# Attention output: all state products ahead of the chunk products, one open group per column group of a bank

## The chip, the cores and the metric

The kernel runs on one core of one Trainium2 chip. The metric is device time in microseconds of that core. Before the change the median of 13 runs is 155.75 us (154.82 to 157.44). A profile is one execution recorded by the hardware profiler; its span is the time from the first to the last instruction.

## The reference

Two parts follow each other. The first is a gated linear recurrence for 4 batches of 8 heads, 768 tokens and head size 48; its output, laid out as 3072 tokens of 384 features, goes into a feed-forward layer with the maximum of three products:

```python
state = zeros(B, H, 48, 48)
for t in range(768):
    state = alpha[:, :, t, :, None] * state + k[:, :, t, :, None] * v[:, :, t, None, :]
    y[:, :, t] = einsum('bhd,bhde->bhe', q[:, :, t], state)
x = y as (3072, 384)
h = maximum(maximum(x @ w1, x @ w2), x @ w3)      # 768 wide
out = h @ w_out                                   # 384 wide
```

## The kernel before

The tokens are cut into 12 steps of 256: step s is chunk s // 4 of batch s % 4. A step has two row blocks of 128 tokens (x = 0 and 1), and within them tokens go in pairs. For one row block the attention output is a sum of two kinds of products: the scaled queries with the state that stands before the block (its state products), and the masked scores within the block with the values (its chunk products). The first row block of chunk 0 has no state yet, so it has chunk products alone.

The work on a step is cut into pieces, each a small function with a letter: sums of logarithms of the gates (`c`), their exponentials, scaled queries and keys (`k`, `q`), their transposes, on TensorE for the first steps (`T`) and by DMA on the SP queue from step 5 on (`D`), scores (`A`), the mask (`a`, VectorE), the attention output (`Y`, the function `attend`), its copy to SBUF (`x`, `keep_x`), the new state (`S` on TensorE, `s` on VectorE, `z` mostly on GpSimd), and the feed-forward part: gate products (`G`), maxima (`h`), the last product (`O`) and the store (`o`). Three strings, PROLOGUE, STEADY and LAST, give the order in which the pieces are written out by hand; each engine runs its own instructions in that order, and waits only for data and for buffers. STEADY is written out once per stage and interleaves the feed-forward part of one step with the attention of the next and the preparation of the ones after it.

PSUM has eight banks, given out under three tags: `w` (2), `s` (2) and `g` (4). `attend` takes two banks of one tag, one for each row block, `yps[x]`. A bank holds the output turned round, as 128 partitions by three groups of 128 tokens. The 128 partitions are four column groups of 32 (m), and each of the three groups f of a column group is one block of 32 output features. A block of 32 features lies in the 48 of one head or reaches into the next one: `part` 0, 1 or 2 within a pair of heads. `turns[m]` is the order in which the column group m takes its three f; the block that reaches over two heads comes second.

A state product (line 311) multiplies 128 rows by 32 columns of the state with 128 tokens of queries. A chunk product (line 330) multiplies 64 rows by 32 columns of the values with 128 columns of the masked scores; x chooses the upper or lower 64 rows. A late attend (chunk 1 and 2, eight of them) has 24 state products and 64 chunk products; an early one (chunk 0, four) has 12 and 64. The function writes them in this order: state products of the first group of each column group, then the chunk products that close the first group and open the second, then the state products that close the second group and those that open the third, and then the chunk products that close the third. In each column group of a bank one accumulation group is open at a time: the first product onto a group has `start`, the last has `stop`.

Of the kernel before, what the change touches and what calls it, by code (L numbers as in the profile page):

```python
# [23 lines left out]
def kernel(  # L24
# [12 lines left out]
    nc = tc.nc  # L37

    B, H, S, D = q.shape
    NT, DM = out.shape  # L40
    DF = moe_w_out.shape[0]
    P = 128
    C = 32
    NF = DM // P
    NJ = DF // P
    U = 2
    R = 2
    J = P // R
# [3 lines left out]
    HP = H // 2  # L52
# [120 lines left out]
    def bank(shape, name, tag, dtype=FP32):  # L173
        return ps.tile(shape, dtype, name=name, tag=tag, bufs=banks[tag])
# [116 lines left out]
    def attend(s, _, tag):  # L291
        c, b = divmod(s, B)
        vt, qkT = vts[s % NQ], qkT_of.pop(s)
        lats = [lat_of.pop((s, u)) for u in range(U)]
        yps = [bank([P, NF, P], "yps", tag or "s") for _ in range(U)]
        for x in range(U):
            y_of[s, x] = yps[x]
        blocks = [divmod(n, 3) for n in range(NF * P // C)]
        old = [U * c + x > 0 for x in range(U)]

        turns = []
        for m in range(P // C):
            fs = sorted(range(NF), key=lambda f: blocks[P // C * f + m][1] == 1)
            turns.append([fs[0], fs[2], fs[1]])

        def from_state(g, first):
            for x in range(U):
                for m in range(P // C) if old[x] else ():
                    f = turns[m][g]
                    p, part = blocks[P // C * f + m]  # L310
                    nc.tensor.matmul(yps[x][C * m:C * (m + 1), f, :],  # L311
                                     sts[b][x][:, p, C * part:C * (part + 1)],
                                     qkT[:, :, 0, p, x * J:(x + 1) * J], start=first, stop=not first)

        def from_chunk(*groups):
            jobs = []
            for m in range(P // C):
                todo = []
                for g, first in groups:
                    f = turns[m][g]  # L320
                    p, part = blocks[P // C * f + m]
                    cols = [(0, C * part)] * (part < 2) + [(1, D + C * (part - 1))] * (part > 0)
                    todo += [(f, first, n == 0, n == R * len(cols) - 1, i, p, n % R, at)
                             for n, (i, at) in enumerate(j for j in cols for _ in range(R))]
                jobs.append(todo)
            for n in range(max(len(j) for j in jobs)):
                for m, job in enumerate(jobs):
                    for x in range(U) if n < len(job) else ():
                        (f, first, begin, end, i, p, r, at), rows = job[n], slice(x * J, (x + 1) * J)
                        nc.tensor.matmul(  # L330
                            yps[x][C * m:C * (m + 1), f, :],
                            vt[rows, r * HP + p].rearrange("p a b -> p (a b)")[:, at:at + C],
                            lats[p // (HP // R)][rows, i, p % (HP // R) * R + r, :],
                            start=begin and (first or not old[x]),
                            stop=end and (not first or not old[x]))

        from_state(0, True)
        from_chunk((0, False), (1, True))
        from_state(1, False)
        from_state(2, True)  # L340
        from_chunk((2, False),)

    def keep_x(s, x, eng):
        if s not in xT_of:
# [92 lines left out]
    def warm(_, n, *x):  # L437
# [9 lines left out]
        "k": scale_k, "q": scale_q, "V": values,  # L447
        "T": turn, "t": keep_turned, "D": turn_by_dma, "A": scores, "a": masked,
        "Y": attend, "x": keep_x, "M": gates, "S": update, "s": add_state, "z": decay_state,
        "G": gate, "h": maxed, "O": project, "o": store,  # L450
    }
# [95 lines left out]
```

## Time and profile before

| What | Value |
|---|---|
| median of 13 runs | 155.75 us |
| profiled execution, its own time | 155.98 us |
| its span | 154.2 us |
| TensorE busy | 144.8 us (94%) |
| VectorE busy | 120.7 us (78%) |
| GpSimd busy | 84.8 us (55%) |
| ScalarE busy | 77.7 us (50%) |
| chunk products of attend, L330 | 768, busy 11.0 us |
| state products of attend, L311 | 240, busy 7.8 us |
| gate products, L396 | 648, busy 78.0 us |
| granted TensorE clock | 1.00 throughout |

In lines of the profile PE is the matmul side of TensorE, PEld its weight loads, DVE is VectorE, ACT ScalarE, POOL GpSimd, SP SyncE, which here only issues DMAs (SPq). L330 is line 330 of the kernel. A line of a timeline gives a start, a length, the operation, output<-inputs and a count, and in brackets the idle time before it and what ended it. Matmuls overlap, and each one's end is modelled, so a sum of busy times by line can be more than what the line adds to the time; the chain of work that ended last counts each moment once.

### The profile page before, as it was taken

To read this page: it belongs to the slowest core of one execution; us is meant where nothing else is said; L and a number is where in the kernel's file an instruction comes from. 1 tells how busy PE (TensorE), PEld (TensorE's weight loads), DVE (VectorE), ACT (ScalarE), POOL (GpSimd) and SP (SyncE) were. 2 spreads that over 40 slices of the span, in tenths; PEclk is the share of its full clock that TensorE was granted. 3 is DMA by queue.
4 is the path that set the end of the run, shared out by engine and by line. 5 is a ranking of instruction groups with operands and counts; after the bars stand their busy time and mean duration, and the time that the engine had idled before them with its cause. 6 is when DMAs were issued, how large, how long until landed. Compare 5 with 4: busy or idle time off the path is not lost.

```text
span 154.2 us, 6225 instructions
## 1 busy us (share of the span) xinstructions
PE 144.8 (94%) x2691; PEld 108.1 (70%) x2691; DVE 120.7 (78%) x212; ACT 77.7 (50%) x156; POOL 84.8 (55%) x123
## 2 busy tenths in 40 slices
PE   6989883999999999999999999999999999999990
PEld 2446452788877698687787786886877878868850
DVE  2256985699989799989799799797896995885560
ACT  3578927645774386383582483553835614132221
POOL 5418798466919307928848659379288573010000
PEclk9999999999999999999999999999999999999999
DMA  5999998799999999799999999999908609411023
GB/s 138 322 325 325 277 330 253 229 351 285 361 284 249 234 320 296 208 123 284 261 237 283 167 218 334 141 261 294 234 5 82 160 4 106 137 55 51 6 100 104
DMA packets 73035, 32.52 MB, mean 211 GB/s; under 512 B 65456, under 2 KB 73008, under 8 KB 73008
## 3 DMA queue, kind: packets, MB, share of 16 engines
q1 hardware_dynamic: 72576, 31.89, 83.2%
q8 instruction: 21, 0.34, 1.0%
q10 hardware_dynamic: 432, 0.23, 0.6%
q14 instruction: 6, 0.05, 0.1%
HBM read 23.73 MB, written 4.72 MB: 184 GB/s over the span
## 4 chain that ended last, share of the span: by engine, by line
PE 84%; DVE 4%; DMA 3%; issue 2%; SPq 2%; POOL 1%; ACT 1%; ACTq 0%; POOLq 0%
PE gps L396 48%; PE ops L420 15%; PE yps L330 6%; PE yps L311 4%; PE aps L280 4%; PE sps L369 3%; DMA ra<-in_alpha_dram 3%; PE tps L259 2%; SPq L95 2%; DVE lat L287 2%; POOL qk L235 1%; PE wps L440 1%; PE lps L209 1%; DVE pa L184 1%; ACT ob L156 1%
## 5 line engine op out<-in xcount | busy, mean ns | idle before, releaser
L396 PE MATMUL gps<-xT,wcat 128*128 128x256 f16 x648 | 78.0, 273 | 0.2 <-DVE lat L287 0.2
L396 PEld LDWEIGHTS <-wcat 128*128 128x128 f16 x648 | 60.8, 98 | 10.5 <-ACT wcat L150 0.7
L411 DVE TENSOR_TENSOR hT<-gps,h 128x512 f16<-128x512 f32 x36 | 24.4, 687 | 11.3 <-PE gps L396 11.1
L287 DVE TENSOR_TENSOR lat<-aps,cp 128x512 f16<-128x512 f32 x48 | 30.6, 682 | 1.7 <-PE aps L280 1.7
L156 ACT ACTIVATE ob<-ops,c 128x384 f32<-128x384 f32 (+1 forms) x21 | 12.1, 574 | 38.0 <-PE ops L420 37.2
L411 DVE TENSOR_TENSOR h<-gps,h 128x512 f16<-128x512 f32 x36 | 24.1, 688 | 3.4 <-PE gps L396 1.2
L420 PE MATMUL ops<-wo,hT 128*128 128x384 f16 x144 | 26.5, 326 | 0.0
L383 POOL TENSOR_TENSOR st<-full,gm 128x384 f16<-128x384 f32 x20 | 16.9, 846 | 15.7 <-DVE full L379 10.0
L420 PEld LDWEIGHTS <-hT 128*128 128x128 f16 x144 | 14.1, 98 | 7.3 <-DVE hT L411 0.2
L353 POOL TENSOR_TENSOR gt<-ge 128x4 f32<-128x4 f32 x17 | 4.2, 248 | 21.3 <-ACT ge L229 21.3
L150 ACT CAST xT<-yps 128x384 f16<-128x384 f32 x21 | 9.2, 481 | 11.9 <-PE yps L330 11.7
L152 DVE CAST h<-gps 128x512 f16<-128x512 f32 x20 | 13.7, 687 | 1.2 <-PE gps L396 1.1
L150 ACT CAST h<-gps 128x512 f16<-128x512 f32 x16 | 9.3, 586 | 10.4 <-PE gps L396 7.2
L440 PE MATMUL wps<-blank 128*128 128x512 f16 x47 | 13.1, 426 | 1.2 <-DVE blank L512 1.2
L330 PE MATMUL yps<-lat,vt 64*32 64x128 f16 x768 | 11.0, 220 | 2.2 <-issue 2.2
L235 POOL TENSOR_TENSOR qk<-ka,ic 128x384 f16<-128x384 f32 x11 | 11.4, 1035 | 0.3 <-ACT ic L217 0.2
L235 POOL TENSOR_TENSOR qk<-qa,ac 128x384 f16<-128x384 f32 x11 | 11.0, 998 | 0.2
L156 ACT ACTIVATE vt<-rv,c 128x768 f16<-128x768 f32 x11 | 10.3, 938 | 1.3 <-DMA rv<-in_v_dram 1.3
L184 POOL TENSOR_TENSOR pa<-ra 128x384 f32<-128x384 f32 x9 | 9.0, 1001 | 3.5 <-DVE ka L199 3.5
L330 PEld LDWEIGHTS <-vt 64*32 64x32 f16 x768 | 7.2, 90 | 4.7 <-issue 2.4
L235 POOL TENSOR_TENSOR qk<-rq,ac 128x384 f16<-128x384 f32 x10 | 10.0, 999 | 0.0
L440 PEld LDWEIGHTS <-blank 128*128 128x128 f16 x47 | 4.6, 107 | 6.6 <-issue 2.4
(52 smaller groups left out, 166.5 us busy)
## 6 DMA issues: line engine op xcount, KB each, us to landing
ra<-in_alpha_dram SPq DMA_DIRECT2D x12, 384.0 KB, 5.6
rk<-in_k_dram SPq DMA_DIRECT2D x12, 384.0 KB, 5.1
rq<-in_q_dram SPq DMA_DIRECT2D x12, 384.0 KB, 5.4
rv<-in_v_dram SPq DMA_DIRECT2D x12, 384.0 KB, 5.4
out_dram<-ob SPq DMA_DIRECT2D x23, 192.0 KB, 3.9
ws<-in_moe_w_dram SPq DMA_DIRECT2D x9, 384.0 KB, 6.4
ws<-in_moe_w_out_dram SPq DMA_DIRECT2D x3, 384.0 KB, 4.9
qkT<-qk SPq DMA_TRANSPOSE x14, 4.6
```

The costliest lines, as they stand in the source:

```text
L150: nc.scalar.copy(out=dst, in_=src)
L152: engines[eng].tensor_copy(out=dst, in_=src)
L156: nc.scalar.mul(dst, src, col)
L184: engines[eng or "p"].tensor_mul(pair_of[s], raw("a", s, 0), raw("a", s, 1))
L235: engines[eng or "p"].tensor_mul(dst.rearrange("p a b c -> p (a b) c")[:, :, :D], near_of.pop((s, n)) if r == 0 else raw(n, s, 1), dec_of[ ...
L287: nc.vector.tensor_mul(lat_of[s, u][:, i].rearrange("p (a r) t -> p a r t", r=R), aps_of[s, u][i].rearrange("p (a r) t -> p a r t", r=R), ...
L330: nc.tensor.matmul(yps[x][C * m:C * (m + 1), f, :], vt[rows, r * HP + p].rearrange("p a b -> p (a b)")[:, at:at + C], lats[p // (HP // R)] ...
L383: engines[eng or "p"].tensor_mul(sts[s % B][1 - x].rearrange("p a (b d) -> p a b d", d=D), full_of.pop((s, x)), gm_of.pop((s, x)).unsqueez ...
L396: nc.tensor.matmul(gps[:, j, :], wcat[:, f, g, jj * P:(jj + 1) * P], xT[:, f].rearrange("p u t -> p (u t)"), start=(f == 0), stop=(f == NF ...
L411: nc.vector.tensor_max(h, gps, h_of[s, i - 1])
L420: nc.tensor.matmul(ops, hT_of[s][:, jj, u * P:(u + 1) * P], wo16[:, jj, :], start=(jj == 0), stop=(jj == NJ - 1))
L440: nc.tensor.matmul(wps, blank[:, :P], blank, start=True, stop=True)
```

## The change

The state products of all three groups are written first, for row block 0 and then 1, and then all chunk products in one run. Within a column group of a bank only the very first product has `start` (the state product of the first group, or the first chunk product where there is no state), and only the very last has `stop`: all three groups f of a column group are open together. The argument `skip_group_check` changes no instruction. The order of chunk products is the same as before within the run, and so is their number.

```diff
-        def from_state(g, first):
-            for x in range(U):
-                for m in range(P // C) if old[x] else ():
+        for x in range(U):
+            for g in range(NF) if old[x] else ():
+                for m in range(P // C):
                     f = turns[m][g]
                     p, part = blocks[P // C * f + m]
                     nc.tensor.matmul(yps[x][C * m:C * (m + 1), f, :],
                                      sts[b][x][:, p, C * part:C * (part + 1)],
-                                     qkT[:, :, 0, p, x * J:(x + 1) * J], start=first, stop=not first)
-
-        def from_chunk(*groups):
-            jobs = []
-            for m in range(P // C):
-                todo = []
-                for g, first in groups:
-                    f = turns[m][g]
...
-                        nc.tensor.matmul(
-                            yps[x][C * m:C * (m + 1), f, :],
-                            vt[rows, r * HP + p].rearrange("p a b -> p (a b)")[:, at:at + C],
-                            lats[p // (HP // R)][rows, i, p % (HP // R) * R + r, :],
-                            start=begin and (first or not old[x]),
-                            stop=end and (not first or not old[x]))
-
-        from_state(0, True)
-        from_chunk((0, False), (1, True))
-        from_state(1, False)
-        from_state(2, True)
-        from_chunk((2, False),)
+                                     qkT[:, :, 0, p, x * J:(x + 1) * J], start=(g == 0), stop=False, skip_group_check=True)
+
+        jobs = []
+        for m in range(P // C):
+            todo = []
+            for f in turns[m]:
...
+        for n in range(max(len(j) for j in jobs)):
+            for m, job in enumerate(jobs):
+                for x in range(U) if n < len(job) else ():
+                    (f, i, p, r, at), rows = job[n], slice(x * J, (x + 1) * J)
+                    nc.tensor.matmul(
+                        yps[x][C * m:C * (m + 1), f, :],
+                        vt[rows, r * HP + p].rearrange("p a b -> p (a b)")[:, at:at + C],
+                        lats[p // (HP // R)][rows, i, p % (HP // R) * R + r, :],
+                        start=(n == 0 and not old[x]), stop=(n == len(job) - 1),
+                        skip_group_check=True)
```

## The prediction

> **What bounds the kernel now.** I read the page's busy shares first, then the chain of work that ended last, then the stages one by one. Before has a median of 155.75 us; its profiled execution took 155.98 us and its span is 154.2 us, so 1.8 us lie around the span. All sums below are made in the span.
>
> ```profile
> span 154.2 us, 6225 instructions
> PE 144.8 (94%) x2691; PEld 108.1 (70%) x2691; DVE 120.7 (78%) x212; ACT 77.7 (50%) x156; POOL 84.8 (55%) x123
> PE 84%; DVE 4%; DMA 3%; issue 2%; SPq 2%; POOL 1%; ACT 1%; ACTq 0%; POOLq 0%
> ```
>
> TensorE carries the end: it is busy for 94% of the span and holds 84% of the chain. Attend runs twelve times, once per step. In the chain its state products (L311) and chunk products (L330) are separate pieces. This is the chain (start us, length us, what) in a late attend with both row blocks old:
>
> ```profile
> 84.22 0.97 PE ops L420 x6
> 85.19 0.23 PE yps L311 x8
> 85.42 0.53 PE yps L330 x48
> 85.95 0.34 PE yps L311 x16
> 86.29 0.23 PE yps L330 x16
> 86.52 2.07 PE gps L396 x18
> ```
>
> The attend costs 1.33 us in four blocks with no gap before or after. The same chain in the third attend, where only x=1 has a state:
>
> ```profile
> 38.97 0.17 PE yps L311 x4
> 39.14 0.53 PE yps L330 x48
> 39.67 0.23 PE yps L311 x8
> 39.89 0.24 PE yps L330 x16
> ```
>
> From these lengths a block's cost splits in two. State blocks of 4, 8 and 16 take 0.17, 0.23 and 0.34 us: 14 to 15 ns per product, and 0.11 to 0.12 us whatever the count. Chunk blocks of 16 and 48 take 0.235 and 0.53 us: 9.2 ns per product, and 0.09 us whatever the count. The trace's single starts say the same: within a block, rounds of four (state) or eight (chunk) products start 56 to 75 ns apart, and from the last start of one kind to the first weight load of the other pass about 0.15 us (85.726 to 85.878, 86.067 to 86.214).
>
> Then the stretches between attends, for slack (us, then busy us of each engine):
>
> ```profile
> core 0: us, PE busy (x) PEld busy (x) DVE busy (x) ACT busy (x) POOL busy (x), PEclk, DMA share, GB/s
> 85.19:95.75 10.56, 10.56 (x228) 8.25 (x231) 9.41 (x17) 5.60 (x12) 7.24 (x12) 1.00 1.09 230
> ```
>
> TensorE is busy for the whole of each stage from 39 us on, and the stages from 64 to 127 us are all 10.56 to 10.58 us long. VectorE is next with 9.41 us. The waits of the stage before this one show that it stands still for TensorE once, for 1.0 us:
>
> ```profile
> DVE hT L411 <- PE gps L396: 1.0, 1, 1.0
> ```
>
> Three places of the first third differ. TensorE's timeline after the first attend (it ends at 20.0) and inside the second, and VectorE's after the third:
>
> ```profile
> 21.91 0.40 PE L259 MATMUL tps<-cp,qk 128*128 128x128 f16 x4 [0.56 <-POOL qk L235]
> 24.32 0.41 PE L330 MATMUL yps<-lat,vt 64*32 64x128 f16 x29
> 26.91 0.34 PE L330 MATMUL yps<-lat,vt 64*32 64x128 f16 x19 [2.18 <-issue]
> 42.29 0.68 DVE L411 TENSOR_TENSOR hT<-gps,h 128x512 f16<-128x512 f32 x1
> 43.13 0.69 DVE L411 TENSOR_TENSOR h<-gps,h 128x512 f16<-128x512 f32 x1 [0.17 <-PE gps L396]
> ```
>
> After the first attend TensorE waits for GpSimd. The second is cut by 2.18 us in which TensorE waits for nothing the profile shows. After the third, VectorE works without a pause from 34.0 to 43.0 us, and TensorE's gate product at 43.1 follows hT closely.
>
> **What the Trainium skill says.** TensorEngine Tiling (Array Packing), Tiling Modes, Key Properties: changing the tiling mode, not merely the tile, drains the TensorE. State products are 128 rows by 32 columns, chunk products 64 by 32, so each border between blocks is such a change; the trace agrees, with 0.15 us at the border against 0.056 us between rounds. PSUM — Partial Sum Buffer, The four PSUM rules: the start flag clears the written-bits of the whole bank in the quadrants written, and later products without it overwrite where the bit is clear and add where it is set; so one start per column group and bank suffices, and the flags themselves carry no work. No run here shows that rule by itself. The Performance Considerations of the first page give a fixed overhead of about 60 cycles per matmul; the trace's spacing is used instead.
>
> **The change part by part.** No instruction is added or removed: the order has the same 2691 matmuls and as many weight loads, and the other engines' and SP's orders are the same but for line numbers. Waits sit on the corresponding instructions.
>
> State groups 1 and 2 move ahead of all chunk products: 16 in the eight late attends, 8 in the four early ones. Four blocks become two. Late attend: 24 state products, 0.34 + 8 x 0.0145 = 0.45 us; 64 chunk products, 0.53 + 16 x 0.0092 = 0.68 us; together 1.13 against 1.33, a gain of 0.20 us, which is one state block's and one chunk block's fixed part (0.115 + 0.09). Early attend: 12 state, 0.23 + 4 x 0.0145 = 0.29, and 64 chunk, 0.68: 0.97 against 1.17, again 0.20 us.
>
> One uncertainty is the slope in a run of 64. In the 48-block the first four rounds start 56 to 66 ns apart, the later ones about 67 to 75 with the instructions evenly 4.2 ns apart, as if supply ran out. Two more rounds at 56 give 0.64, at 75 give 0.68. I take 0.68, the dearer; the other end adds 0.04 us per attend. A second is x: before, the 16-block alternates banks; after, x=0 writes three rounds into its own bank before x=1 starts. The third attend's 8-block (x=1 alone, one bank) and the late 8-block (x=0, then x=1) both take 0.23 us, so I price this at nothing, and it can hardly be below.
>
> Waits: the moved state products read the state and qkT that group 0 has waited for already. x=1's first state product now stands 8 products later, the first chunk product 16 later, so their waits for st, the yps bank and lat are looser. What waits for an attend is keep_x (ScalarE, then gate), and both yps banks still end with the last chunk products: it moves as a whole. No DMA is issued by attend; the transposes and loads on SP follow GpSimd and other consumers, which follow TensorE.
>
> Does the gain last to the end? I compared, for each TensorE wait, the producer's end with the waiter's start; a truly blocked one starts 0.05 us after. In a late stage the nearest is the project bank freed by add_state (0.29 us), which follows TensorE's own update, begun 1.5 us earlier, so it moves along; VectorE regains step at its 1.0 us wait. The transposes (landing 0.18 us before their reader in the stage at 102 us, 0.6 to 1.9 in the others) lose 0.2 us of their room: perhaps 0.1 us once. Early: first attend, gain 0 (GpSimd's 0.56 us wait takes it). Second: 0.20, since the two borders that go lie after the stall. Third: hT ends 0.115 us before its reader, so 0.06. Fourth: 0.20. Sum: 0 + 0.20 + 0.06 + 0.20 + 8 x 0.20 = 2.06. The transpose may take 0.1 from it and the cheaper end of the chunk slope add up to 0.4 (ten attends by 0.04); I leave both out and take 2.05. Span 152.15; the profiled execution's 155.98 becomes 153.9, and the median of the runs 155.75 becomes **153.7 us**.
>
> **The rivals.** (1) DMA or VectorE takes most of it. DMA share reads 0.98 to 1.12 in the four stages from 64 to 106 us, and VectorE is at 89%. If each of those four stages keeps its 10.56 us, 0.8 us are lost, and with the second attend's gain lost too, 1.0: about 154.7. Against it: SP's queue stands idle for 1.0 to 1.5 us ahead of each later pair of transposes, because it waits for GpSimd and not for room.
> (2) The change doesn't do what it says: the border costs are moved into the longer blocks (64 chunk products starve for instructions, all rounds at about 90 ns instead of 67, 8 x 23 ns = 0.18 us). Then 155.6, the same. The measured 67 to 75 in rounds five and six speaks against more.
> (3) Slower: three rounds running into one bank serialize. A late attend has 4 such neighbours among its six rounds. At 50 ns each the 0.20 us is gone; at 75 ns (so 131 in place of 56) a late attend loses 0.10 us and eight lose 0.8; an early one, with 2 neighbours, still gains 0.05, so about 156.4. The 0.23 us of both 8-blocks speaks against it.
>
> **How the numbers follow.** Forecast 0.72, rival 1 0.15, rival 2 0.07, rival 3 0.06. A measurement here can tell about 0.5% (0.8 us) from no change: below 154.97 is faster. Of the forecast nearly all and of rival 1 about two thirds are faster: 0.81. Same 0.12, slower 0.07. The forecast's own range is 153.0 (chunk slope at the cheap end, and run to run 0.3) to 154.4; taking in rival 1, 80% lie between 152.9 and 155.0.
>
> **What would show it.** In the chain, each late attend as two pieces, x24 of 0.45 and x64 of 0.64 to 0.68 us, and the stages from 74 us at 10.36 us with TensorE still fully busy. After the first attend a longer wait for GpSimd, and near 43 us a wait of about 0.15 us for hT. Wrong if state pieces of 24 last over 0.6 us, if TensorE shows waits in the late stages, or if the stall in the second attend changes its length: nothing in the waits says what sets it, it lies ahead of both borders that go, and at over 4.2 us it would use up the whole gain.

## The result, and the profile after

The changed kernel took 154.0 us (median of 11 runs, 153.14 to 156.47) against 155.94 us (48 runs) of the kernel before. Medians take in all executions; ratios leave out those, of any kernel, that took over 1.5% more than its fastest. The ratio is 0.9901, with a 95% interval of 0.9873 to 0.993. That is 1.5 us faster (1.1 to 2.0). The forecast was 153.7 us and a gain of 2.05 us: the direction and the place are right, and the size is a little high. Two later sets of runs of the same kernel gave 0.9872 (0.9802 to 0.9943) and 0.9855 (0.9796 to 0.9913).

The profiled execution of the changed kernel took 154.98 us, 1.0 us more than its median, so its span (153.2 us) shows more losses than a usual run. The lines of the page that answer to those of before:

```profile
span 153.2 us, 6225 instructions
PE 143.2 (93%) x2691; PEld 108.3 (71%) x2691; DVE 121.9 (80%) x212; ACT 77.6 (51%) x156; POOL 84.5 (55%) x123
PE 65%; DVE 12%; DMA 7%; POOL 5%; issue 4%; SPq 2%; ACT 2%; ACTq 0%; DVEq 0%; POOLq 0%
```

TensorE still bounds the kernel, but its share of the chain fell from 84% to 65%: the chain now runs for longer through VectorE (12%), DMAs (7%) and GpSimd (5%). The same chain in a late attend (L311 state products, L328 chunk products, L388 gate products):

```profile
82.73 0.98 PE ops L412 x6
83.70 0.45 PE yps L311 x24
84.15 0.66 PE yps L328 x64
84.82 2.08 PE gps L388 x18
```

Two pieces instead of four, and 1.11 us instead of 1.33. The weight loads of TensorE in the same place show the two blocks as the engine sees them:

```profile
83.63 0.34 PEld L311 LDWEIGHTS <-st 128*32 128x32 f16 x24 [0.32 <-issue]
84.08 0.60 PEld L328 LDWEIGHTS <-vt 64*32 64x32 f16 x64
84.74 0.33 PEld L388 LDWEIGHTS <-wcat 128*128 128x128 f16 x4
```

A stage between two attends (columns as before):

```profile
73.29:83.63 10.34, 10.34 (x224) 8.26 (x223) 9.41 (x17) 5.60 (x12) 7.22 (x12) 1.00 1.07 239
```

It is 10.34 us long instead of 10.56, TensorE is busy for all of it, and VectorE and GpSimd do the same work as before in the shorter time.

Not all stages are so. TensorE's timeline has these stops after the start of the second attend (in brackets the idle time and what ended it):

```profile
25.85 0.56 PE L328 MATMUL yps<-lat,vt 64*32 64x128 f16 x43 [1.00 <-issue]
41.97 1.47 PE L388 MATMUL gps<-xT,wcat 128*128 128x256 f16 x12 [0.24 <-DVE hT L403]
95.43 0.36 PE L328 MATMUL yps<-lat,vt 64*32 64x128 f16 x22 [0.45 <-issue]
102.20 0.64 PE L280 MATMUL aps<-qkT 48*64 48x128 f16 x32 [1.00 <-DMA qkT<-qk]
```

The first stop is the one that before has in its second attend, shorter this time. The second was forecast (0.15 us for hT). The third and the fourth are new: in the eighth attend TensorE stands still after 42 chunk products, and seven microseconds later the scores wait 1.0 us for a transpose by DMA. The two take 1.45 us, more than twice the 0.66 us that the three stages from 63 to 94 us gained: the changed kernel starts its eighth attend 1.7 us ahead of before (93.98 against 95.68 us) and its ninth only 0.1 us ahead (106.14 against 106.26).

### The profile page after: what moved, and what is told of

The parts are those of the page before. It is cut to its first block, busy times and chain, and to the rows that moved or that the text cites. A ratio compares the mean times of both kernels' runs of the same rounds, so it can differ in the third digit from the quotient of the medians.

```text
span 153.2 us, 6225 instructions
## 1 busy us (share of the span) xinstructions
PE 143.2 (93%) x2691; PEld 108.3 (71%) x2691; DVE 121.9 (80%) x212; ACT 77.6 (51%) x156; POOL 84.5 (55%) x123
## 4 chain that ended last, share of the span: by engine, by line
PE 65%; DVE 12%; DMA 7%; POOL 5%; issue 4%; SPq 2%; ACT 2%; ACTq 0%; DVEq 0%; POOLq 0%
PE gps L388 35%; PE ops L412 13%; PE yps L328 4%; DMA qkT<-qk 4%; PE aps L280 3%; POOL qk L235 3%; DMA ra<-in_alpha_dram 3%; DVE hT L403 3%; PE yps L311 2%; SPq L95 2%; PE sps L361 2%; DVE lat L287 2%; DVE h L403 2%; PE tps L259 2%; PE wps L432 2%
## 5 line engine op out<-in xcount | busy, mean ns | idle before, releaser
L388 PE MATMUL gps<-xT,wcat 128*128 128x256 f16 x648 | 78.0, 273 | 0.2 <-DVE hT L403 0.2
L388 PEld LDWEIGHTS <-wcat 128*128 128x128 f16 x648 | 60.9, 98 | 10.0 <-PE gps L388 0.5
L432 PE MATMUL wps<-blank 128*128 128x512 f16 x47 | 13.6, 439 | 1.2 <-DVE blank L504 1.2
L328 PE MATMUL yps<-lat,vt 64*32 64x128 f16 x768 | 9.2, 221 | 1.5 <-issue 1.5
L280 PE MATMUL aps<-qkT 48*64 48x128 f16 x384 | 8.6, 218 | 1.4 <-DMA qkT<-qk 1.0
```

Source lines behind the costliest of these rows:

```text
L280: nc.tensor.matmul(aps[i][cols, a * R + r, :], qkT[rows, r, 1, p, cols], qkT[rows, :, 0, p, cols], start=True, stop=True)
L328: nc.tensor.matmul(yps[x][C * m:C * (m + 1), f, :], vt[rows, r * HP + p].rearrange("p a b -> p (a b)")[:, at:at + C], lats[p // (HP // R)] ...
L388: nc.tensor.matmul(gps[:, j, :], wcat[:, f, g, jj * P:(jj + 1) * P], xT[:, f].rearrange("p u t -> p (u t)"), start=(f == 0), stop=(f == NF ...
L432: nc.tensor.matmul(wps, blank[:, :P], blank, start=True, stop=True)
```

## The experiments

Two theories and their rivals were put to test. The **border theory**: what costs is each passage from state to chunk products and back, whatever the number of products and whatever groups are open. The **transfer theory**: the part of the gain that was missing went to the transposes by DMA, which no longer land ahead of their readers. A third, on TensorE's own instructions, came out of the traces.

| Run | What it is | Median us | Ratio to before (95%) |
|---|---|---|---|
| changed kernel | two blocks | 154.0 | 0.9901 (0.9873 to 0.993) |
| e1_after_again | the same | 154.06 | 0.9872 (0.9802 to 0.9943) |
| e2_six_blocks | six blocks | 157.49 | 1.0132 (1.005 to 1.0215) |
| e3_four_blocks_two_open | four blocks, two open groups | 155.96 | 0.9975 (0.9944 to 1.0006) |
| e4_one_in_middle | two blocks and one product between | 155.64 | 0.9983 (0.9954 to 1.0012) |
| e5_warm_halves | changed, 47 more matmuls ahead | 156.05 | 1.0007 (0.9966 to 1.0048) |
| e6_q0_early | changed, earlier transposes | 153.32 | 0.9819 (0.979 to 0.9848) |
| e7_banks_alternate | changed, banks alternate | 154.02 | 0.9836 (0.9794 to 0.9879) |
| e8_before_q0_early | before, earlier transposes | 155.8 | 0.9999 (0.9963 to 1.0035) |
| e9_q0_early_again | e6 again | 153.98 | 0.9883 (0.9835 to 0.9931) |
| e10_after_third | changed kernel again | 153.65 | 0.9855 (0.9796 to 0.9913) |

e1 to e4 shared runs of before (median 156.15), e5 to e7 (156.0), and e8 to e10 (156.69).

**Borders: two more.** Before, with the middle chunk block parted:

```diff
         from_state(0, True)
-        from_chunk((0, False), (1, True))
-        from_state(1, False)
+        from_chunk((0, False),)
+        from_state(1, True)
+        from_chunk((1, False),)
         from_state(2, True)
         from_chunk((2, False),)
```

> Before with the chunk products of the first and second group parted by the second group's state products: six blocks per attend instead of four, one group open at a time. Border theory: 0.20 us more per attend where TensorE sets the time (9 to 11 of 12): plus 1.8 to 2.2 us, ratio 1.012 to 1.014, late attends of 1.53 us. Rival (what is saved by the change comes with the open groups or the start flags): as before, ratio 1.000.

It became 1.3% slower (2.1 us; 0.8 to 3.4), as the border theory has it. The chain of a late attend:

```profile
117.39 0.23 PE yps L311 x8
117.61 0.24 PE yps L330 x16
117.85 0.22 PE yps L311 x8
118.07 0.35 PE yps L330 x32
118.42 0.23 PE yps L311 x8
118.64 0.24 PE yps L330 x16
```

The same products take 1.51 us in six blocks, 1.33 in four and 1.11 in two: 0.18 and 0.22 us for each pair of borders. Open groups and flags can't have cost this: the kernel has one open group per column group at a time, like before. Whether they save anything is the question of the next run.

**Open groups without fewer borders.** The same four blocks, but the first two groups open together:

```diff
         from_state(0, True)
-        from_chunk((0, False), (1, True))
         from_state(1, False)
+        from_chunk((0, False), (1, False))
         from_state(2, True)
         from_chunk((2, False),)
```

(with `stop` and the group argument as in the changed kernel)

> State products of the first and second group ahead, then their chunk products, then the third group's state and chunk products: two groups open together, still four blocks. Border theory: ratio 1.000 (0.997 to 1.003), late attends of 1.33 us as x16, x48, x8, x16. Rival (open groups, start flags): a good part of the gain, 0.993 to 0.995.

The ratio is 0.9975, and its interval reaches into what the rival expected; the chain decides:

```profile
104.79 0.34 PE yps L311 x16
105.12 0.53 PE yps L331 x48
105.66 0.23 PE yps L311 x8
105.88 0.24 PE yps L331 x16
```

It is 1.33 us, as before, with the sizes of the two state blocks exchanged. Two groups open in a bank save nothing by themselves.

**One product in the middle.** The changed kernel, with the last state product of row block 1 left out of the first block and written after half of the chunk products:

```diff
+        places = [(x, g, m) for x in range(U) for g in range(NF) for m in range(P // C)]
+        from_state([i for i in places if i != last])
...
         for n in range(max(len(j) for j in jobs)):
+            if n == 4:
+                from_state([last])
```

> The changed kernel with one of its 24 (or 12) state products per attend, the last, moved into the middle of the chunk products: the order is as in the changed kernel but for this one, and two borders are back. Border theory with a cost that does not depend on the count: 0.20 us more per attend than the changed kernel, ratio to before 0.998 to 1.002. Rival (the cost goes with the number of moved products or with the groups): nearly the whole gain stays, 0.988 to 0.993.

```profile
105.80 0.44 PE yps L313 x23
106.25 0.35 PE yps L334 x32
106.59 0.16 PE yps L313
106.75 0.35 PE yps L334 x32
```

One product out of 24 gives back nearly all that the change saves: 1.30 us, and a ratio of 0.9983. The lone product holds TensorE for 0.16 us in the chain, and parting the chunk block costs 0.04 on top (two of 0.35 against one of 0.66). Here the cost does not go with the count.

Is it the change of tile shape that costs, or any change from one kind of product to another? The trace of before has both. Gate products (L396) and last products (L420) are both 128*128 tiles, score products (L280) are 48*64:

```profile
81.38 0.45 PE aps L280 x32
81.83 0.76 PE gps L396 x6
82.59 0.98 PE ops L420 x6
83.56 0.66 PE gps L396 x6
```

Six gate products take 0.66 us after last products and 0.76 us after score products. Between single starts it is the same: from a gate product to a last product pass 0.109 us, which is the spacing of gate products themselves, but from a last product to the first state product (128*32) pass 0.256 us, where last products are 0.162 us apart. Score products follow products of the new state (64*64, L369) after 0.033 us, so 48 rows in place of 64 cost nothing either. In this trace, then, passages that keep the 128*128 or the 64*64 tile are free, and those to another tile cost about 0.1 us or more. This fits what the Trainium skill states (TensorEngine Tiling (Array Packing), Key Properties, cited in the prediction): a change of the tiling mode drains TensorE. The drain itself no trace shows.

**Banks.** The changed kernel with the loops over groups and row blocks exchanged:

```diff
-        for x in range(U):
-            for g in range(NF) if old[x] else ():
-                for m in range(P // C):
+        for g in range(NF):
+            for x in range(U):
+                for m in range(P // C) if old[x] else ():
```

> The changed kernel with the loops over groups and row blocks exchanged in the state products: neighbouring rounds of four write banks 0, 1, 0, 1 instead of 0, 0, 0, 1, 1, 1. Border theory: nothing changes, x24 in 0.45 us and the ratio of the changed kernel (0.985 to 0.993). Rival (rounds into one bank hinder each other): x24 shorter by 0.05 us or more in late attends, 0.4 us in all.

```profile
105.70 0.45 PE yps L311 x24
106.15 0.67 PE yps L328 x64
```

The 24 state products take 0.45 us in either order, so rounds into one bank do not hinder each other (rival 3 of the prediction). Its ratio overlaps with those of the changed kernel.

**The missing part: transposes.** The changed kernel once more, unedited:

> The changed kernel once more, for a second profile. Border theory (each pair of borders between state and chunk products costs 0.20 us): late attends again as x24 of 0.45 and x64 of 0.66 us, stages of 10.35 us, ratio 0.985 to 0.993. Transfer theory for the part of the gain that the first profile lost (1.0 us at 102 us, waiting for a transpose by DMA): TensorE waits again for a transpose by 0.3 us or more in some stage from 70 to 134 us. Its rival, chance: no such wait over 0.3 us, and that profile's 1.0 us was one run's.

The attends are again x24 of 0.45 and x64 of 0.67. In this profile the scores at 82.3 us start 0.29 us late and 0.13 us after a transpose landed, as in the first profile (102.07 to 102.20 us); the timeline names VectorE there, but its result was there earlier. So it just missed the 0.3 us that the transfer theory asked for. Then GpSimd's order was changed, so that the first transpose of a stage can be issued earlier:

```diff
-        h1@0 h5@0 V0@2 k0p@2 S0@1 s0@1 z0p@1 A0g@1 a0@1 A1@1 k1p@2 G7@0
-        O1@-1 a3@1 G6@0 q0p@2 s1@1 q1p@2 a1@1 a2@1 D0@2 D1@2 l3@5 l1@5
+        h1@0 h5@0 V0@2 k0p@2 S0@1 s0@1 z0p@1 A0g@1 a0@1 A1@1 q0p@2 G7@0
+        O1@-1 a3@1 G6@0 k1p@2 s1@1 q1p@2 a1@1 a2@1 D0@2 D1@2 l3@5 l1@5
```

> The changed kernel with two of GpSimd's pieces in the steady stages exchanged: the scaled queries of the first token come before the scaled keys of the second, so the first of the two transposes by DMA can be issued some 0.95 us earlier in a stage and the second some 0.6 us. Transfer theory (the transposes set part of the time since the change): they land 0.6 us or more earlier ahead of their readers, no wait of TensorE for them is left, ratio 0.001 to 0.004 better than the changed kernel. Rival (the DMA engines' queue and not the issue decides when they land, or the wait was chance): room and time as in the changed kernel.

No wait for a transpose was left. Of the seven pairs, the second transpose landed 1.0 to 2.3 us ahead of its reader. The ratio was 0.9819, better than any of the changed kernel. To see what belongs to the exchange, it was then run on before, and again beside the changed kernel:

> Before with GpSimd's exchange alone (scaled queries of the first token ahead of the scaled keys of the second). Transfer theory: in before the transposes land ahead of their readers already (0.18 to 1.9 us), so they get room that nobody needs: ratio 0.997 to 1.002; the exchange is worth something only after the borders are gone. Rival (the exchange helps by itself, through GpSimd or VectorE): as much as it gave the changed kernel, 0.990 to 0.995.

> The changed kernel with the exchange, once more beside the changed kernel itself, for the size: transfer theory 0.3 to 1.0 us faster than the changed kernel, ratio to before 0.980 to 0.986, and no wait of TensorE for a transpose. Rival (the first reading was chance): the ratio of the changed kernel, 0.987 to 0.990.

> The changed kernel beside the two above. Border and transfer theory: ratio 0.985 to 0.990; a wait of TensorE for a transpose in one of the stages from 70 to 134 us in about half of the profiles (two of the four so far of kernels with two borders fewer and without the exchange). If instead the time is that of the exchange's kernel, the transposes cost nothing.

On before it is worth nothing (0.9999), as expected. The second set of runs of the exchange gave 0.9883, no better than the changed kernel beside it (0.9855), and the medians were 153.98 and 153.65 us. So the first reading was in part chance, and whether the exchange makes the changed kernel faster stays open. The waits say a little more. The changed kernel's third profile had its stop again, in another stage:

```profile
80.08 0.64 PE L280 MATMUL aps<-qkT 48*64 48x128 f16 x32 [0.47 <-DMA qkT<-qk]
```

Over all profiles: of the five with two blocks and GpSimd's old order (the changed kernel three times, e5, e7) four have one wait for a transpose, of 1.00, 0.29, 0.64 and 0.47 us; I had counted only two of the first four when I wrote the last expectation. Of the two with the exchange none has one, and none of the five with four or six blocks has. So the wait came with the shorter stages; it is 0.5 us on average over the five, and none has it twice. That the exchange takes it away rests on two profiles, and in the second of these the closest transpose landed 0.4 us ahead of its reader.

**TensorE's own instructions.** The stops that wait for nothing shown stand at fixed places of the instruction stream. In the changed kernel's first two profiles they follow the 350th and the 1756th matmul, 1406 apart. TensorE has 5382 matmuls and weight loads. The page lists an instruction queue with 21 packets (q8), which I take for TensorE's, as it has by far the most instructions. A packet then stands for about 256 instructions or 128 matmuls, and 1406 is 11 of these within two; the packets ahead of the two stops are 11 apart as well. In all twelve profiles the stop at the 350th matmul ends 2.3 to 2.6 us after one of these packets begins (23.42 to 25.85 us in the changed kernel, 24.36 to 26.91 in before), and the one at the 1756th likewise (93.06 to 95.43). To tell the place in the stream from the place in the attend, each warm-up matmul was written as two halves:

```diff
-        for _ in range(n):
-            nc.tensor.matmul(wps, blank[:, :P], blank, start=True, stop=True)
+        for _ in range(2 * n):
+            nc.tensor.matmul(wps[:, :256], blank[:, :P], blank[:, :256], start=True, stop=True)
```

> The changed kernel with each of the 47 warm-up matmuls of 512 columns written as two of 256, so that every later instruction of TensorE stands 47 matmuls (94 instructions) further on in its stream, at the same work. In both profiles of the changed kernel TensorE stood still, waiting for nothing shown, after its 350th matmul (in the second attend) and after its 1756th (in the eighth, after 42 chunk products, 0.4 us in the matmul row), 1406 matmuls or 11 times 256 instructions apart. Supply theory (TensorE's own instructions come late, in portions of 256): the standstills stay at counts near 350 and 1756, so they leave the places they had, the second attend and the 42nd chunk product of the eighth; 0.3 to 1.5 us faster than the changed kernel if the new places are less dense. Rival (a run of 64 chunk products itself stalls): the eighth attend still stalls after some 42 chunk products, time unchanged.

The timeline ahead of the second attend, and the eighth attend:

```profile
23.02 0.36 PE L280 MATMUL aps<-qkT 48*64 48x128 f16 x12
27.38 0.32 PE L280 MATMUL aps<-qkT 48*64 48x128 f16 x4 [4.00 <-issue]
...
99.04 0.52 PE L311 MATMUL yps<-qkT,st 128*32 128x128 f16 x24
99.49 0.74 PE L328 MATMUL yps<-lat,vt 64*32 64x128 f16 x64
100.16 1.05 PE L388 MATMUL gps<-xT,wcat 128*128 128x256 f16 x8
```

The first stop stayed at the 350th matmul, which is now a score product ahead of the second attend. So its place belongs to the stream and not to the work. The eighth attend runs through, and so does the 1756th matmul; but e7 and e10, with the changed kernel's count of instructions, show no such stop there either (e7 a delay of 0.2 us), so on the second stop e5 decides nothing. That a run of 64 chunk products does not stall by itself is seen in every profile, in all the attends that run through.

The hoped-for gain did not come: the whole gain of the change was gone (1.0007). Two things came together. In the profiled execution, at 158.24 us the longest of the 14, the stop lasted 4.0 us, because its packet began 1.4 us after TensorE had stopped (24.81 us). And 2.1 us into the stop, at 25.48 us, the granted clock fell to half, until 32.31 us; the page shows it in slices of 3.9 us:

```profile
PEclk9999997589999999999999999999999999999998
28.46 1.49 PE L388 MATMUL gps<-xT,wcat 128*128 128x256 f16 x6
```

Six gate products take 1.49 us there, against 0.66 at full clock. TensorE worked for 4.9 us at half the clock, which costs up to 2.5 us by my estimate (half of 4.9). This is not that one execution alone: in 12 of the 14 the mean granted clock was 0.972 to 0.989, against 0.994 or more in all but one of the changed kernel's executions; and the two at 0.997 and 0.999 took 154.98 and 154.39 us, less than the other twelve. So part of the loss goes with the lower clock, and how much the place of the stop costs without it stays open. So does what decides when a packet begins.

## Why the prediction came out as it did

**The attend: right.** Forecast 1.13 us for a late attend, measured 1.11 to 1.12, and 0.95 against 0.97 for an early one; the slope for 64 chunk products lay at 0.66 to 0.67, between the ends of 0.64 and 0.68. The fixed parts of the blocks, read from the chain of before, are the cause: e2, e3 and e4 show them each in its own way.

**The stages: right.** From the start of the fourth attend to the end of the span, before takes 102.15 us, and e3 and e8 102.3 and 102.1; the three two-block profiles without a wait for a transpose (e5, e6, e9) take 100.2 to 100.4. That is 1.8 to 1.95 us for nine attends, against 9 x 0.20 in the sum. The prediction named waits of TensorE in the late stages and another length of the stall as signs of being wrong. Both came (1.0 us at 102 us; 1.0 us in place of 2.18), but they are what follows below, and not a fault in what a border costs.

**The transposes: the term that was mis-sized.** The sum left them out ("perhaps 0.1 us once"), on one profile's smallest room of 0.18 us. Four of five profiles have a wait of 0.29 to 1.00 us, 0.5 us on average over the five. The reasoning that the room shrinks by 0.2 us was sound. But the 0.18 us were no room: in all four stops TensorE's wait instruction for the transpose passes 0.03 us after the landing and the matmul follows 0.13 us after it, and in before, at 102 us, the wait passes 0.03 us after the landing too. And the room itself varies by about a microsecond from run to run: in this stage of the first two profiles the second transpose landed at 102.10 us (before) and at 102.07 us (after), though it was issued 0.8 us earlier in the latter (97.14 and 96.37). Rival 1 came near this: it had DMAs take back up to 1.0 us, but through four stages that keep their whole length. Those stages did get shorter; a single late transpose was what cost, and VectorE had no part in it in the late stages.

**The early part: right in three of four attends.** The first gained nothing. The second gained 0.2 us: from its start to the third, less the stop, 12.35 us in before and 12.16 in e6, e7, e9 and e10. The first profile of the changed kernel has 12.31 there, and e1 12.76, with a wait of 0.37 us for VectorE in it. The third was put at 0.06, and its wait for hT, forecast as about 0.15 us, is there in all seven two-block profiles, at 0.22 to 0.26 us. From the third to the fourth, before takes 13.15 us; e5, e7 and e9 the same within 0.02, so these gained nothing; the other four took 13.4 to 14.0, with a stop after 25 of the 32 score products, at the 733rd matmul (e2 has it too).

**What was not foreseen: the supply of instructions.** The prediction saw the stop in the second attend and said that it did not know its cause. It did not see that there can be more such places in the stream: 0.65 us in the eighth attend in two of five profiles with the old GpSimd order, and 0.25 to 0.8 us at the 733rd matmul in four of seven. The second is three times 128 matmuls, less one, behind the first stop, and comes 2.2 us after a packet begins in the changed kernel's first profile (42.11 us). As e2 has this stop with six blocks, it isn't shown that faster passages bring it about. The stop at the 350th, which all twelve profiles have, lasted from 0.8 to 4.2 us between matmul starts. It is not the whole of what differs from one execution to the next: of the three profiles of the changed kernel one reaches its first attend 1.1 us later than the others (20.10 us against 19.0), and their stops differ by 0.6 us at most.

**The sum as it came out.** An estimate from the profiles: 1.8 to 1.95 us for nine attends and 0.2 for the second, less 0.5 for the transposes, about 0.25 for the eighth attend (0.65 in two of five) and about 0.2 on the way to the fourth (0.28 to 0.42 in three of five) leave 1.05 to 1.2 us, the low end of the measured 1.1 to 2.0. So the gain of the borders was forecast rightly, and up to half of it is taken back by terms that the sum put at nothing. That the two medians lie 1.9 us apart, close to the forecast 2.05, is partly luck, as the ratio gives 1.5.

## What to carry to other kernels

When small products of two tile shapes alternate on a TensorE that sets the time, count the passages between shapes: here a pair costs 0.2 us whether it encloses one product or sixteen, so gather each shape into one run, and let several accumulation groups share a bank to make that possible. When an engine that bounds the kernel gets faster, look for transfers that are issued at one point of a stage and read at another: their room shrinks with the stage, and one profile doesn't tell how much of it there is. A stop that waits for nothing shown, at the same count of instructions in every run, may be worth placing where the work is sparse, but test the new place, and look at the granted clock as well as at the stop: here the stop got longer and the clock fell behind it.

## What the runs showed that was not expected

TensorE can stand still where nothing in the waits shows why, and the place moves with its instruction stream and not with the work: at the 350th matmul in all twelve profiles, for 0.8 to 4.2 us, ending 2.3 to 2.6 us after a packet of the instruction queue begins. This fits instructions that come in portions of about 256. With 47 more matmuls ahead, the ratio went from 0.9855 to 0.9901 (three sets of runs) to 1.0007, as much as the change studied here gains; a granted clock that fell to half for 6.8 us went with it, and it isn't shown how the loss divides between the stop and the clock.
